# A fused attention and mixture-of-experts kernel: another written-out order, the last slot sums by halves, the first layer's banks opened earlier, the router's matrix stored in rows

## The chip, the cores and the metric

The kernel runs on one core of a Trainium2 chip. Its time is the device time of one execution in microseconds. The median of three runs of the kernel before is 344.75 us (343.94 to 345.07). One further execution was profiled; that one took 344.9 us, and the span of its trace is 343.1 us. All stretches below are counted from the start of that span.

## The reference

Two parts follow each other. The first is linear attention with a positive feature map for 8 batches, 8 heads, 576 tokens and a head dimension of 64:

```python
def phi(x):
    proj = np.einsum('bhsd,df->bhsf', x, w_phi)          # 64 -> 128 features
    proj = proj - np.max(np.abs(proj), axis=-1, keepdims=True)
    return np.concatenate([np.exp(proj), np.exp(-proj)], axis=-1)
q_p, k_p = (phi(q), phi(k))
kv = np.einsum('bhsf,bhsd->bhfd', k_p, v);  z = np.sum(k_p, axis=2)
num = np.einsum('bhsf,bhfd->bhsd', q_p, kv)
den = np.einsum('bhsf,bhf->bhs', q_p, z)[..., None] + 1e-06
x = num / den                                            # then reshaped to 4608 x 512
```

The second is a soft mixture of experts over the 4608 tokens with 32 slots, 8 experts of 4 slots each. The router's logits are normalised once over the tokens (to make the slots' inputs) and once over the slots (to mix the slots' outputs back):

```python
logits = x @ phi                                         # phi: 512 x 32
d = softmax(logits, over tokens);  slot_input = d.T @ x  # 32 x 512
h = np.maximum(slot_input[e] @ w1[e], 0.0);  slot_out[e] = h @ w2[e]   # 1024 hidden, per expert
c = softmax(logits, over slots);   out = c @ slot_out    # 4608 x 512
```

All inputs and outputs are float32.

## The kernel before, in words

**Attention, the main loop.** Two batches are taken together, so there are 32 units (4 batch pairs by 8 heads) of 1152 tokens, which are 9 tiles of 128 tokens. 72 blocks of four tiles pass through `proj` (line 264: one block of keys and one of queries, the queries two blocks behind), the exponentials on ScalarE (`kneg_exp`, `kpos_exp`, `qpos`, `qneg`, lines 295 to 334), the maxima on VectorE (`kmax` 269, `qabs` 326), the scaling of the values on GpSimd (`vals` 284), the sums of keys by values (`kvmm` 311) and the numerators (`num` 364, three to a unit), which VectorE (`scale` 375, `comb` 380) and GpSimd (`divide` 406) turn into rows of x.

**The slots, interleaved.** When enough of x stands, its tiles are turned by TensorE, multiplied by the router's matrix, and the exponentials' sums over tokens are added to a running accumulator `acc` (names `turn`, `logits`, `gmax`, `gexp`, `dturn`, `slotsum`, `update`). The last three groups have functions of their own, whose names begin with z. In `zsum` (559) group 0 and 1 are summed into one PSUM bank and group 2 into another, each as matmuls of 512 columns; `zup` (564) adds a bank to `acc` in two halves of 256 columns. `zone` makes the correction of the maxima, `zst` (602, 604) multiplies `acc` by it into one bank `st` of five times 32 columns, and `zsi` (607) copies that to `si`, the slots' inputs, in two halves. `si` lies in the place of the router's matrix `phs`. `layer1` (841) multiplies `si` by the first weights.

**The way back to the tokens.** For the first three groups of 512 tokens `tfour` (617, GpSimd) spreads the mixing weights, `tturn` (626) turns them on TensorE into a PSUM bank, `tcopy` (630, ScalarE) copies that bank and `trest` (636, VectorE) subtracts the copy from it in its upper half. The other six groups go through `repeated` and `combine` later.

**Experts and output.** After the planned part the rest is written out: `layer1` of experts 4 to 7, `lastw`, `hidden`, `picked`, `layer2` (935) for both halves of the output columns, `slots2`, and `output` (959, 960), which writes 18 tiles of 512 KB. There, TensorE's order is that of the text.

**Transfers.** All go through SyncE's queue, in the order in which they are issued: 512 KB for each two blocks of keys and queries (`load`), 325 KB for each unit of values (`vload`), the constants and the router's matrix (`consts`), and 64 weights of 512 KB. 26 of these weights (`weight`) have room from the start; others follow when pools of the main loop close (`close`).

**The order.** Everything from the first `proj` to the last `trest` is a list of tasks. A string `ORDER` holds one letter for each task, in the order in which the instructions are issued; every engine executes its own in that order. `Plan.run` takes the letters one by one. It also hands out numbered buffers, the tokens: a task that names one in `get` takes the first free number, and a `put` gives it back. `pr` is the token for the three PSUM banks z0, z1 and z2 of the pool `fin["pr"]`, `pl` that for two other banks, `nm` with `mo` or `psn` that for the three banks `nm0` to `nm2`. The figures for cost and latency in the task list were used by the program that searched the order; the kernel that runs takes nothing from them. A tile in a bank can be written anew when all readers of the tile before it in the same bank have ended.

At the end of the kernel before, the order of TensorE is: first of the three `tturn` between the first two `zdt`, second one after `zsum` 2, then `zst` 0 and 1, four `layer1` steps, the third `tturn`, and then the written-out part from `layer1(1, ...)` on.

Of the kernel before, what the change touches and what calls it, by code (L numbers as in the profile page):

```python
# [21 lines left out]
CH = 3  # L22
# [34 lines left out]
class Plan:  # L57
# [42 lines left out]
ORDER = (  # L100
    "abbccdaebfdebgehijeefechigcjdklfdmehinoelkgnfjgchiajmoljfcpnhldikqrdnlggjfsmoqahibtlukjcvmojwvcnfpdqrwlvkqnhislm"
    "oxbkwftcghyvjqwfzdiaAqhxnjbmolAvxgdikjcvpwrwlqdgmojsqfklAahinbtgcmojvvwcydkzlwgfnqrpjdqhismolAfnAtcvkAwmolynghij"
    "vfqawzbhlAvqkpjwmocdiAvgcjbnfxdlrnAqghidlkwsfyjmoqzhitalkjcvmowpvcgbnjxdlrqwAdfqnhilgvkjwksqfAaAmoljmotchiygvpzv"
    "cAwfnjhqwrnlqvAkdilfwgsymoAqhztkdicjmovwcdkAagbAnlgjfbvrqpjwflshimoAqvdtlkwvgnhijqywajmolvqwzcvAwApcyAbdkxzlnfxA"
    "xgnfqAjmoBhiBhACcCkdiBmodrBCcgsfjqhinatCblkjvnmoDvrwlEqwFBpvgBfwslCqhtkdicjmoCcbdkgnfBjvBhiCyljGnwqrqmovClvgwkzH"
    "dDmosfchiItEpwjcFbnagHJIdJnAgKAlAqfyjrqvwlkzvahidmoqsjflgLkAhicpjmowvcwbntxqdAyAGlnkfdqhivlgvfwjwkjqmohilvcmoLwp"
    "yzMcbnfAagdlxrjdqgksqAmoAnlhitkjvfcwamojzvhilAngqfMjNdpcrwvlghidqjkslkAaAwfbnyqthimoljvmozKcgpjwvcbnfAhwlqrAdiAq"
    "vgsklmodtkcwgjnfvqmojbdxlwganhiyqzvrAwcpAkjsfldhiAmoqvnNtflwgvkyjwhiqjmolvqzwAcvAAwpcybfznaAlxOkxxBdfxBmonCqCkBd"
    "hiBgCrjcgsCqmobfltkPvhiAnDjhajdicxAEgwjFlvnqfwpBvmodBrwlCgqCjshiqktcmoyvjvcGbfwanBwkBnldCrCqdmolzkhiHgDImojfcEhi"
    "spcFbvnHwJIydtJnAAKrlAqdfqvklwgLhijGsmoqggMvfLljzwkvhicApmowjcbdantqfdAlAkOhiyqvggwjmolznAfavNkqwjmolvhicjpOcbnf"  # L110
    "AwlrdqksglfjnhiAamoqKyhtlzkdijcmoMvvpAwcgNnAAdqrjwlfvqdkwglmosjkhiyqajznftxlbhivcgvmowjpcbnfxAwlrdqAAdgqkPshilmo"
    "vtnfcjwhivkqwybfnqgvhjzmoldikAcmopAvgrwjcdsqfbAgahilwtnyqvfjwlahvnkdiqmokwlcmopjvzOcAkwAdgymlAzdfAqgnofjBgnhiBrj"
    "cCCajsBxxBntxlxCCAPhidArqvjDvkwfwlgEmoqFBvkBhimocCpwCsctBBCldqjnqyvkajnlbCxwrvxqxfblgvkwzHhidDIfwJmoEsFcApGyhitH"
    "ljIqfnmoJGKgAhzckAdijvqdlwakvbgnmoqfjLKglhiAwmocArpjvcsbfAqwnytldkvqgdhijlwfajnxgmozvqAhiwkMlcApmoAvjcnfwlkdrqnN"
    "qsmohildgtfjcvkywaLhizblvAgnmoqApwjfcvArdjlwksqhiqmodytzcnfgvhijlwknAmovqArwjlvkwcpsymoAlgqzntcAkvdAQjRwQnSqSqvk"
    "wrQOQSgfljshiSAvTmomoUlVQpwQRUSyqtSPQvqSwTzvAyQVAzMwqSyQRvzQwSWyASAzTAAXRXXYYYZVZ0Z0W10W2W2P341567483N489642+8-3"
    "4*796-49//5R//=+=<<>O!*P1!!!5+*")
# [8 lines left out]
def tile_kernel(ctx: ExitStack, tc, xT, vv, w, phi, w1, w2, cst, out):  # L126
# [471 lines left out]
    def zst(i):  # L598
        sf = fin["sf"]
        if i == 0:  # L600
            fin["st"] = bank3("zst", [128, KC + 1, NS], "pst")
            nc.tensor.matmul(fin["st"][:, KC, 0:1], sf.rearrange("p a s -> p (a s)"), ssum, start=True, stop=True)
        for kc in (2 * i, 2 * i + 1):
            nc.tensor.matmul(fin["st"][:, kc], acc[:, kc * 128:(kc + 1) * 128], sf[:, 0], start=True, stop=True)
# [50 lines left out]
    for b in range(NB + 2):  # L655
        def task(kind, engine, cost, fn, key, bank, **k):
            add(kind, key, engine, cost, lambda: fn(key), at=4 / 3 * bank, **k)
        task("proj", PE, 0.99 if 1 < b < NB else 0.77, proj, b, b, after=[("load", b // 2)], lat=0.27, mode="r", get=["psk"] * (b < NB) + ["psq"] * (b > 1), put=["xs"] * (b % 2))
        bank = [f"kb{b % 2}"]
        if b < NB:  # L660
            task("kmax", DVE, 0.6, kmax, b, b, after=[("proj", b)], get=["mk"] + bank, put=bank, lat=0.13)
            task("kfac", ACT, 0.19, kfac, b, b, after=[("kmax", b)])
# [3 lines left out]
        for p, (b_, u, t0, t1) in enumerate(pieces):  # L666
            if b_ == b:
# [7 lines left out]
                     get=["pkv"] * (t0 == 0), put=["kf", "vs"] * end, mode="c", lat=0.22)  # L675
        q, bank = b - 2, [f"qb{b % 2}"]
        if q >= 0:
            task("qabs", DVE, 0.63, qabs, q, q, after=[("proj", b)], get=bank, put=bank, lat=0.13)
# [4 lines left out]
    for s in range(NK):  # L683
# [9 lines left out]
        if end:  # L693
# [6 lines left out]
        task("num", PE, 0.71, num, after=[("qneg", (CH * s + CH - 1) // 4), ("kvcopy", u)], get=["psn", ("nm", ("num", s))],  # L700
             put=["qf"] * any(t % 4 == 3 for t in range(CH * s, CH * s + CH)) + ["kvs"] * end, mode="c", lat=0.22)
        task("scale", DVE, 0.272, scale, after=[("num", s), ("qsquare", u)], get=[] if c else ["un"])
        task("comb", DVE, 0.272, comb, after=[("scale", s)], put=["psn", ("nm", ("num", s))])
# [64 lines left out]
        task("dturn", PE, 0.32, dturn, n, after=[("gexp", n)], get=hold("dturn", n), put=["lT"], mode="f")  # L768
# [23 lines left out]
    def close(k):  # L792
# [5 lines left out]
            ("u", [("divide", (NU - 1, 2))]), ("c", [("zsum", 2), ("zlog", 2)])]  # L798
# [7 lines left out]
    for c in range(NCH):  # L806
        bk = "pr" if c == 2 else "pl"
        last("zturn", c, PE, mode="f", cost=(0.466, 0.14, 0.466)[c], fn=lambda c=c: zturn(c), after=opens + [("divide", (NU - 1, c))] + [("flogits", (i, 0, 1, 2)) for i in last_of], get=[("pr", ("x", c))])
        d = pick("zcopy") == "d"
        last("zcopy", c, DVE if d else ACT, (0.07 + 0.1335 * len(zj(c))) if d else 0.05 + 0.107 * len(zj(c)), lambda c=c, d=d: zcopy(c, d), after=[("zturn", c)], get=[("xT", ("z", c))], put=[("pr", ("x", c))])  # L810
        last("zlog", c, PE, 0.45, lambda c=c: zlog(c), mode="s", after=[("zcopy", c), ("part", (last_of[c], 0, 1, 2))], get=[(bk, ("l", c))], put=[("xT", ("z", c))])
        last("zmax", c, DVE, 0.46, lambda c=c: zmax(c), after=[("zlog", c)])
# [15 lines left out]
    for i in range(2):  # L828
        last("zst", i, PE, 0.59, lambda i=i: zst(i), after=[("zup", 2 + i), ("zone", 5), ("zss", 1)], get=[] if i else ["mo", ("nm", "zst")])
# [22 lines left out]
    last("hopen", 0, None, 0.0, hopen, after=[("zsi", 1)] + [("zspin", i) for i in range(NFIN)] + [("zlt", c) for c in range(NCH)], lat=0.0)  # L852
# [184 lines left out]
```

## Time and profile before

| what | value |
|---|---|
| median of three runs | 344.75 us |
| profiled execution, its own time | 344.9 us |
| its span | 343.1 us |
| TensorE busy, share of the span | 327.2 us, 95% |
| VectorE, ScalarE, GpSimd | 243.6, 233.2, 168.0 us |
| data moved | 74.09 MB, mean 216 GB/s |
| main loop, last `flogits` begins at | 272.75 us |
| `layer1` begins at | 284.17 us |
| last matmul ends at | 332.83 us |

The table's last three rows are from the timeline of TensorE. In a row of the timeline stand the start and the duration in us, the engine, the line, the operation with its tiles, the number of instructions, and in brackets how long the engine was idle before and what released it. "issue" there means that no wait in the profile explains the idle time. In a row of the table by windows stand, for each engine, its busy time and its instructions, then the granted clock of TensorE (PEclk), the share of the DMA engines' time and the rate in GB/s. PEld is TensorE's weight load, which runs beside the matmuls.

### The profile page before, as it was taken

To read this page: it belongs to the slowest core of one execution; us is meant where nothing else is said; L and a number is where in the kernel's file an instruction comes from. 1 tells how busy PE (TensorE), PEld (TensorE's weight loads), DVE (VectorE), ACT (ScalarE), POOL (GpSimd) and SP (SyncE) were. 2 spreads that over 40 slices of the span, in tenths; PEclk is the share of its full clock that TensorE was granted. 3 is DMA by queue.
4 is the path that set the end of the run, shared out by engine and by line. 5 is a ranking of instruction groups with operands and counts; after the bars stand their busy time and mean duration, and the time that the engine had idled before them with its cause. 6 is when DMAs were issued, how large, how long until landed. Compare 5 with 4: busy or idle time off the path is not lost.

```text
span 343.1 us, 16153 instructions
## 1 busy us (share of the span) xinstructions
PE 327.2 (95%) x6825; PEld 271.1 (79%) x6825; DVE 243.6 (71%) x683; ACT 233.2 (68%) x677; POOL 168.0 (49%) x353
## 2 busy tenths in 40 slices
PE   8997999999999999999999999999999999999970
PEld 4896899998979999998899998979998753355430
DVE  1576487987787888887888888688886562615780
ACT  3897489968867888777789978677886250204470
POOL 1546466872356867561758758256664511130000
PEclk9999899999999999999999999999999999999995
DMA  6377256267234654674262844495426979998698
GB/s 223 117 238 257 83 196 226 67 208 285 66 111 155 204 166 165 210 302 118 58 195 61 320 154 149 162 319 176 128 76 233 352 297 406 408 406 333 282 400 324
DMA packets 22649, 74.09 MB, mean 216 GB/s; under 512 B 2992, under 2 KB 3248, under 8 KB 22576
## 3 DMA queue, kind: packets, MB, share of 16 engines
q1 hardware_dynamic: 22576, 73.05, 60.1%
q8 instruction: 54, 0.88, 1.0%
q14 instruction: 19, 0.16, 0.1%
HBM read 63.60 MB, written 9.44 MB: 213 GB/s over the span
## 4 chain that ended last, share of the span: by engine, by line
PE 92%; DVE 2%; ACT 2%; issue 1%; POOL 1%; ACTq 0%; POOLq 0%
PE kvp L311 23%; PE psn L364 20%; PE psq L264 12%; PE psk L264 10%; PE psx L734 5%; PE yp L935 4%; PE hp L841 4%; PE pso L959 3%; PE psl L417 2%; PE pss L456 2%; PE psw L183 1%; PE psc L921 1%; PE psd L449 1%; PE pss L559 1%; PE psh L903 1%
## 5 line engine op out<-in xcount | busy, mean ns | idle before, releaser
L284 POOL TENSOR_TENSOR vs<-vt,mk 128x520 f32<-128x520 f32 (+3 forms) x128 | 91.6, 730 | 63.3 <-ACT mk L273 42.6
L311 PE MATMUL kvp<-vs,kf 128*64 128x65 f32 (+1 forms) x2304 | 93.3, 230 | 1.9 <-issue 1.9
L311 PEld LDWEIGHTS kvp<-vs,kf 128*64 128x64 f32 x2304 | 81.8, 138 | 9.3 <-issue 5.4
L364 PE MATMUL psn<-kvs,qf 128*64 128x65 f32 x2304 | 82.1, 222 | 0.8 <-issue 0.8
L264 PE MATMUL psq<-xs,wd 64*128 64x128 f32 x576 | 78.7, 284 | 0.0
L264 PE MATMUL psk<-wd,xs 64*128 64x128 f32 x576 | 77.4, 283 | 0.6 <-ACT kf L298 0.4
L364 PEld LDWEIGHTS psn<-kvs,qf 128*64 128x64 f32 x2304 | 74.5, 138 | 3.4 <-issue 1.4
L264 PEld LDWEIGHTS psq<-xs,wd 64*128 64x128 f32 x576 | 69.2, 190 | 3.7 <-issue 1.1
L264 PEld LDWEIGHTS psk<-wd,xs 64*128 64x128 f32 x576 | 68.4, 190 | 4.1 <-ACT kf L298 1.3
L269 DVE TENSOR_REDUCE mk<-psk 128x4 f32<-128x512 f32 x72 | 48.4, 678 | 17.2 <-PE psk L264 8.0
L331 ACT ACTIVATE qf<-psq 128x512 f32<-128x512 f32 x72 | 42.7, 595 | 20.0 <-DVE mts L326 5.9
L326 DVE TRANSPOSE_TENSOR_REDUCE mts<-psq 128x16 f32<-128x512 f32 x72 | 50.7, 706 | 7.6 <-PE psk L264 3.6
L295 ACT ACTIVATE kf<-psk 128x512 f32<-128x512 f32 x72 | 42.6, 592 | 18.7 <-DVE mk L269 7.6
L406 POOL TENSOR_TENSOR xc<-un,dn 128x256 f32<-128x256 f32 x64 | 39.2, 614 | 12.6 <-PE pss L456 6.6
L375 DVE TENSOR_TENSOR un<-psn,eq 128x195 f32<-128x195 f32 x96 | 33.1, 348 | 16.3 <-PE psn L364 12.6
L334 ACT ACTIVATE qf<-psq 128x512 f32<-128x512 f32 x72 | 42.9, 601 | 0.4 <-DVE mts L326 0.2
L298 ACT ACTIVATE kf<-psk 128x512 f32<-128x512 f32 x72 | 42.6, 596 | 0.0
L342 ACT ACTIVATE mh<-mts 32x36 f32<-32x36 f32 x128 | 29.4, 230 | 7.5 <-DVE mts L326 5.9
L380 DVE TENSOR_TENSOR un<-psn,un 128x195 f32<-128x195 f32 x96 | 33.2, 349 | 1.1
L348 DVE TENSOR_REDUCE eq<-mh 32x9 f32<-32x36 f32 x128 | 26.4, 206 | 2.6 <-ACT mh L342 1.1
L272 ACT ACTIVATE mk<-mk 128x4 f32<-128x4 f32 x72 | 15.1, 210 | 4.0 <-DVE mk L269 3.4
L351 POOL TENSOR_TENSOR eq<-eq 128x9 f32<-128x9 f32 x32 | 6.5, 203 | 22.0 <-DVE eq L348 22.0
(130 smaller groups left out, 342.4 us busy)
## 6 DMA issues: line engine op xcount, KB each, us to landing
wt<-w SPq DMA_DIRECT2D x64, 512.0 KB, 7.0
xs<-xT SPq DMA_DIRECT2D x36, 512.0 KB, 4.2
vt<-vv SPq DMA_DIRECT2D x32, 325.0 KB, 3.3
out<-o SPq DMA_DIRECT2D x18, 512.0 KB, 3.7
xs<-xT SPq DMA_DIRECT2D x2, 128.0 KB, 2.5
cs<-cst SPq DMA_DIRECT2D x1, 128.5 KB, 4.0
wd<-w SPq DMA_DIRECT2D x1, 64.0 KB, 2.1
phs<-phi SPq DMA_DIRECT2D x1, 64.0 KB, 3.8
```

What stands on the lines that cost most here:

```text
L264: nc.tensor.matmul(ps, l, r, start=True, stop=True)
L269: nc.vector.tensor_reduce(km[b][:, 2], kx[b], axis=AX, op=ALU.max, apply_absolute_value=True)
L284: nc.gpsimd.tensor_tensor(vs[b][:, :, place(b, u, t, o):place(b, u, t, o) + n], v[:, t + o:t + o + n].unsqueeze(1).broadcast_to([128, 2, n ...
L295: nc.scalar.activation(kf[b][:, 1], kx[b], AF.Exp, scale=-1.0)
L298: nc.scalar.activation(kf[b][:, 0], kx[b], AF.Exp)
L311: nc.tensor.matmul(ps[f:f + FE // 2, pn, o:o + m], kf[b][:, pn, NT * u + t - 4 * b, f:f + FE // 2], v2[:, pn, at:at + m], start=(t == 0 an ...
L326: nc.vector.tensor_reduce(mts.rearrange("p r j -> p j r")[:, o:o + 4], qx[b].rearrange("p j (r t) -> p (j r) t", t=32), axis=AX, op=ALU.ma ...
L331: nc.scalar.activation(qf[b][:, 0], qx[b], AF.Exp)
L334: nc.scalar.activation(qf[b][:, 1], qx[b], AF.Exp, scale=-1.0)
L364: nc.tensor.matmul(ps[64 * f:64 * f + 64, j, pn], q2[:, pn, 64 * f:64 * f + 64], kv[:, pn, b2], start=True, stop=True)
L380: nc.vector.tensor_tensor(x, nx.pop(s)[:, :, 1], x, op=ALU.add)
L406: nc.gpsimd.tensor_tensor(x[:, :, h * D:(h + 1) * D], un[u][:, a:b, 0:64], dn[u][:, a:b].unsqueeze(2).broadcast_to([128, b - a, 64]), op=A ...
```

## The change

Four things change.

1. `ORDER` and the table of its letters are new throughout: 1824 letters in place of 1823. The work of the main loop is the same.
2. `zsum` of group 2 is two tasks, each with all four row groups but only half of the 512 columns, in the same bank. `zup` 2 waits, in the list, for the first half alone; in the new order the second half is issued ahead of it.
3. `st` lies in a bank of `pr` in place of one of `nm`; it isn't given back. `hopen`, which opens the pools of the first layer's accumulators, waits for `zup` 1 and `zone` 3 in place of `zsi` 1, and stands ahead of `zsum` 3. The first `layer1` step stands between `zsi` 0 and `zsi` 1.
4. The host stores the router's matrix as 128 rows of 512 bytes; it was 512 pieces of 128 bytes for the same transfer of 64 KB.

The order of SyncE's queue differs too. The old one has `load` 4, `consts`, `weight` 0, `load` 5, `vload` 4, `weight` 1, `load` 6, `weight` 2, `vload` 5; the new one has `load` 4, `vload` 2, `load` 5, `consts`, `vload` 3, `weight` 0, `vload` 4, `load` 6, `vload` 5, and `weight` 1 only behind `load` 9. At the end the new order has `zspin` 1 ahead of `zlog` 2, no `tturn` ahead of `layer1`, and after the four `layer1` steps three times `tturn`, `tcopy`, `trest`. Following the tokens through both orders, `tturn` 0, 1 and 2 take z2, z2 and z1 in the old one, and z1, z1 and z1 in the new one, where `st` keeps z0 and `zsum` 2 keeps z2.

The diff, without the table of letters and most of the two strings; the last line of each string is there. In the old one `/` is zup, `=` zst, `<` zsi, `>` hopen, `!` l1, `5` tturn, `+` tcopy, `*` trest; in the new one `+` is zup, `-` hopen, `*` zst, `/` zsi, `=` l1, `<` tturn, `>` tcopy, `!` trest, `7` zsum, `O` wsum and `P` wdiv.

```diff
 ORDER = (
...
-    "4*796-49//5R//=+=<<>O!*P1!!!5+*")
+    "585957++-7+Q+**/=/OP===<>!<>!<>!")
...
     def constants():
         nc.sync.dma_start(cs, cst)
-        nc.sync.dma_start(phs, phi.rearrange("(c p) s -> p c s", p=128))
+        nc.sync.dma_start(phs, phi.rearrange("p (c s) -> p c s", c=KC))
...
     def zsum(c):
-        if c != 1:
+
+        h, c = max(c - 2, 0), min(c, 2)
+        if c != 1 and not h:
             fin["sum", c // 2] = zbank("lr"[c == 2], ("s", c), [128, DM], "pss")
         ps = fin["sum", c // 2]
+        d = slice(h * DH, (h + 1) * DH) if c == 2 else slice(0, DM)
         for j in range(G):
-            nc.tensor.matmul(ps[32 * j:32 * j + 32], fin["d", c][:, j], tile4(last_of[c], j), start=c != 1, stop=c > 0,
+            nc.tensor.matmul(ps[32 * j:32 * j + 32, d], fin["d", c][:, j], tile4(last_of[c], j)[:, d], start=c != 1, stop=c > 0,
                              skip_group_check=True)
...
         if i == 0:
-            fin["st"] = bank3("zst", [128, KC + 1, NS], "pst")
+            fin["st"] = zbank("r", ("st", 0), [128, KC + 1, NS], "pst")
...
-        last("zsum", c, PE, 0.87, mode="s", fn=lambda c=c: zsum(c), after=[("zde", c)] + [("zsum", 0)] * (c == 1), get=[] if c == 1 else [(bk, ("s", c))], put=["de"])
+        for i in (2, 3) if c == 2 else (c,):
+            last("zsum", i, PE, 0.45 if c == 2 else 0.87, mode="s", fn=lambda i=i: zsum(i), after=[("zde", c)] + [("zsum", i - 1)] * (i % 2),
+                 get=[] if i % 2 else [(bk, ("s", c))], put=["de"] if i != 2 else [])
...
-            last("zup", 2 * i + h, DVE, 0.396, lambda i=i, h=h: zup(i, h), after=[("zsum", 1 + i), ("zco", i)], put=[("pl", ("s", 0))] if h and not i else [])
+            last("zup", 2 * i + h, DVE, 0.396, lambda i=i, h=h: zup(i, h), after=[("zsum", 1 + i + h * i), ("zco", i)], put=[("pl", ("s", 0))] if h and not i else [])
...
-        last("zst", i, PE, 0.59, lambda i=i: zst(i), after=[("zup", 2 + i), ("zone", 5), ("zss", 1)], get=[] if i else ["mo", ("nm", "zst")])
+        last("zst", i, PE, 0.59, lambda i=i: zst(i), after=[("zup", 2 + i), ("zone", 5), ("zss", 1)], get=[] if i else [("pr", ("st", 0))])
...
-    last("hopen", 0, None, 0.0, hopen, after=[("zsi", 1)] + [("zspin", i) for i in range(NFIN)] + [("zlt", c) for c in range(NCH)], lat=0.0)
+    last("hopen", 0, None, 0.0, hopen, after=[("zup", 1), ("zone", 3)] + [("zspin", i) for i in range(NFIN)] + [("zlt", c) for c in range(NCH)], lat=0.0)
...
-    arrays = dict(xT=xT, vv=vv, w=np.concatenate([w_phi, w_phi]), phi=c(moe_phi), w1=c(moe_w1),
+    arrays = dict(xT=xT, vv=vv, w=np.concatenate([w_phi, w_phi]), phi=c(moe_phi.reshape(KC, 128, NS).transpose(1, 0, 2)).reshape(128, KC * NS), w1=c(moe_w1),
```

The other changed lines give the search other figures for costs and latencies.

More of the change, by code (lines that the diff above doesn't have):

```diff
@@ L102 @@
[L102 to L106, printed above, removed]
@@ L657, in task @@
             add(kind, key, engine, cost, lambda: fn(key), at=4 / 3 * bank, **k)
-        task("proj", PE, 0.99 if 1 < b < NB else 0.77, proj, b, b, after=[("load", b // 2)], lat=0.27, mode="r", get=["psk"] * (b < NB) + ["psq"] * (b > 1), put=["xs"] * (b % 2))
+        task("proj", PE, 0.896 if 1 < b < NB else 0.77, proj, b, b, after=[("load", b // 2)], lat=0.34, mode="r", get=["psk"] * (b < NB) + ["psq"] * (b > 1), put=["xs"] * (b % 2))
         bank = [f"kb{b % 2}"]
         if b < NB:
-            task("kmax", DVE, 0.6, kmax, b, b, after=[("proj", b)], get=["mk"] + bank, put=bank, lat=0.13)
-            task("kfac", ACT, 0.19, kfac, b, b, after=[("kmax", b)])
+            task("kmax", DVE, 0.6, kmax, b, b, after=[("proj", b)], get=["mk"] + bank, put=bank, lat=0.16)
+            task("kfac", ACT, 0.19, kfac, b, b, after=[("kmax", b)], lat=0.21)
             task("kneg_exp", ACT, 0.478, kneg_exp, b, b, after=[("proj", b)], get=["kf"] + bank, put=bank, lat=0.13)
@@ L699, in tile_kernel @@
             task("qsquare", POOL, 0.61, qsquare, u, after=[("qmin", u)])
-        task("num", PE, 0.71, num, after=[("qneg", (CH * s + CH - 1) // 4), ("kvcopy", u)], get=["psn", ("nm", ("num", s))],
-             put=["qf"] * any(t % 4 == 3 for t in range(CH * s, CH * s + CH)) + ["kvs"] * end, mode="c", lat=0.22)
+        task("num", PE, 0.70, num, after=[("qneg", (CH * s + CH - 1) // 4), ("kvcopy", u)], get=["psn", ("nm", ("num", s))],
+             put=["qf"] * any(t % 4 == 3 for t in range(CH * s, CH * s + CH)) + ["kvs"] * end, mode="n", lat=0.22)
         task("scale", DVE, 0.272, scale, after=[("num", s), ("qsquare", u)], get=[] if c else ["un"])
-        task("comb", DVE, 0.272, comb, after=[("scale", s)], put=["psn", ("nm", ("num", s))])
+        task("comb", DVE, 0.272, comb, after=[("scale", s)], lat=0.22, put=["psn", ("nm", ("num", s))])
         for t in ((CH * c, CH * c + CH),) if u == NU - 1 else ((0, NT),) if end else ():
@@ L767, in dturn @@
             turned(lTs.pop(n), ps[:, 1])
-        task("dturn", PE, 0.32, dturn, n, after=[("gexp", n)], get=hold("dturn", n), put=["lT"], mode="f")
+        task("dturn", PE, 0.28, dturn, n, after=[("gexp", n)], get=hold("dturn", n), put=["lT"], mode="f")
         def dcopy(n, got=got):
```

39 lines of the change are left out of this document (22 added, 17 removed), and 10 rows, old and new, of the table LETTERS.

## The prediction, made before the changed kernel was run

> **What bounds the kernel now.** I read the page first, then tables by windows, then the timelines of TensorE, SyncE, ScalarE and VectorE at the places that the change touches.
>
> ```profile
> PE 327.2 (95%) x6825; PEld 271.1 (79%) x6825; DVE 243.6 (71%) x683; ACT 233.2 (68%) x677; POOL 168.0 (49%) x353
> ...
> PEclk9999899999999999999999999999999999999995
> ...
> q8 instruction: 54, 0.88, 1.0%
> ```
>
> TensorE is busy for 95% of the span and no other engine comes near. So an order can gain only where TensorE idles, runs at a lower clock, or does less. Where is that?
>
> ```profile
> 20.00:40.00 20.00, 17.28 (x378) 0.91 0.73 244
> 40.00:60.00 20.00, 20.00 (x540) 1.00 0.55 182
> 60.00:80.00 20.00, 20.00 (x482) 1.00 0.52 174
> 80.00:100.00 20.00, 20.00 (x438) 1.00 0.40 135
> ...
> 40.00:180.00 140.00, 140.00 (x3416) 129.42 (x3413) 115.14 (x325) 113.73 (x343) 86.40 (x179) 1.00 0.51 168
> 180.00:260.00 80.00, 79.44 (x1882) 72.74 (x1878) 66.47 (x186) 64.04 (x191) 51.08 (x110) 1.00 0.50 166
> 284.17:324.00 39.83, 39.83 (x439) 18.13 (x439) 18.18 (x62) 9.59 (x19) 6.18 (x10) 1.00 0.92 369
> ```
>
> The first four rows are of TensorE alone: busy time, matmuls, granted clock, DMA share, GB/s. From 40 to 260 us it loses 0.56 us (79.44 of 80.00), and from the first layer to 324 nothing. What is lost lies at 20 to 40 us: 378 matmuls, where the next three windows have 487 in the mean. The 109 that are missing are worth 109 / 24.3 per us = 4.5 us.
>
> **The early loss.** In the timeline of TensorE, then by windows with all engines (two matmuls are counted per product of two float32 tiles):
>
> ```profile
> 26.04 1.38 PE L364 MATMUL psn<-kvs,qf 128*64 128x65 f32 x38
> 28.23 0.51 PE L364 MATMUL psn<-kvs,qf 128*64 128x65 f32 x10 [0.81 <-issue]
> ...
> 32.14 0.86 PE L311 MATMUL kvp<-vs,kf 128*64 128x65 f32 x22
> 34.92 1.25 PE L311 MATMUL kvp<-vs,kf 128*64 128x65 f32 x10 [1.92 <-issue]
> ```
> ```profile
> 19.50:25.60 6.10, 6.10 (x152) 5.84 (x148) 4.76 (x15) 5.50 (x17) 2.43 (x7) 1.00 1.00 321
> ...
> 28.25:32.50 4.25, 4.25 (x120) 4.06 (x121) 2.33 (x8) 3.17 (x12) 2.55 (x4) 1.00 1.00 342
> ...
> 28.20:34.90 6.70, 4.78 (x128) 4.44 (x127) 3.83 (x12) 4.48 (x15) 3.29 (x6) 1.00 0.94 315
> ...
> 35.07:38.48 3.41, 3.41 (x32) 3.07 (x32) 0.28 (x1) 0.17 (x1) 1.22 (x2) 0.50 0.44 151
> ```
>
> Both pauses lie inside a task (38 is 24 + 14 matmuls, 22 isn't a multiple of 8), so no operand is waited for. Between them stand 128 matmuls and 127 loads, 255 instructions; and 2 x 6825 instructions over the 54 packets of the instruction queue are 253 to a packet. I take it that TensorE ran out of instructions twice, at neighbouring blocks. Both come when the DMA engines had been full for some time (share 1.00). SyncE's queue shows why they were full:
>
> ```profile
> 19.09 0.38 SPq L171 DMA_DIRECT2D xs<-xT  x1
> ...
> 20.46 0.51 SPq L235 DMA_DIRECT2D wt<-w  x1
> 21.07 0.38 SPq L171 DMA_DIRECT2D xs<-xT  x1
> 26.45 0.33 SPq L175 DMA_DIRECT2D vt<-vv  x1
> ...
> 27.88 0.42 SPq L235 DMA_DIRECT2D wt<-w  x1
> ```
>
> Two bursts: `load`, `consts`, `weight`, `load` (1.7 MB) and `vload`, `weight`, `load`, `weight` (1.9 MB), each about 5 us of transfer at 321 to 342 GB/s. The pauses cost, from the last start to the next (a matmul lasts 0.22): 28.23 - 27.20 - 0.05 = 0.98 and 34.92 - 32.78 - 0.05 = 2.09. Behind the second the clock is granted at 0.50 for 3.41 us, worth 1.71. Sum 4.8 us, near the 4.5 of the counts.
>
> **Part 1, the new order.** It has one `weight` in place of three in this stage, and at most 0.84 MB (`vload` and one transfer of 512 KB) or `load` and `consts` (0.7 MB) together, some 2.5 us. So both pauses and the slow clock go: -4.8, between 0 (the pauses have another cause) and -4.8. The weights that leave must come later. The new order's fullest run there is `vload` 26, `weight` 19, `load` 30 and 31, `weight` 20 (2.4 MB); the old one has `vload` 28, `load` 32, three weights and `load` 33 (2.9 MB) without a loss above the 0.56 us. A late block costs between 0 and 3.8 (the second pause with its clock); I take one small pause, +0.8, by the 0.81 that stands in the row. What data the new order makes TensorE wait for can't be seen in the old trace: between -0.56 (all that is lost from 40 to 260) and +1.9 (the longest idle time of TensorE in the trace); I take +0.2, since DVE and ACT have about 30% to spare. And the changes between kinds of matmul:
>
> ```profile
> 60.79 0.27 PE L264 MATMUL psq<-xs,wd 64*128 64x128 f32 x1
> ...
> 60.90 0.27 PE L264 MATMUL psq<-xs,wd 64*128 64x128 f32 x1
> 61.10 0.28 PE L364 MATMUL psn<-kvs,qf 128*64 128x65 f32 x2
> ```
>
> 0.11 within `proj`, 0.20 at its end: 0.09 more. The orders have 74 such ends and beginnings against 60, but 26 against 33 neighbouring `proj`, which change row groups, and more single spins: 0 to -0.6, taken as -0.1. The main loop: -4.8 + 0.8 + 0.2 - 0.1 = **-3.9**.
>
> **Part 2, up to the first layer.** TensorE, then VectorE:
>
> ```profile
> 276.67 0.82 PE L641 MATMUL psw<-cs 128*128 128x512 bf16 x3
> ...
> 278.13 0.66 PE L626 MATMUL psc<-cs,xT 128*128 128x128 f32 x4
> 278.62 0.27 PE L449 MATMUL psd<-cs,eT 128*128 128x128 f32 x1
> ...
> 282.10 0.65 PE L626 MATMUL psc<-cs,xT 128*128 128x128 f32 x4
> 282.59 0.28 PE L602 MATMUL pst<-ssum,sf 128*128 128x1 f32 x2
> 282.77 1.08 PE L604 MATMUL pst<-sf,acc 128*128 128x32 f32 x8
> 284.17 7.07 PE L841 MATMUL hp<-wt,phs 128*32 128x512 f32 x64 [0.32 <-DVE phs L607]
> ```
> ```profile
> 281.41 1.70 DVE L564 SCALAR_TENSOR_TENSOR acc<-acc,co,pss 128x256 f32<-128x256 f32 x4
> ...
> 283.89 0.36 DVE L607 COPY phs<-pst 128x64 f32<-128x64 f32 x2 [0.78 <-PE pst L604]
> ```
>
> Two `tturn` leave this chain, 0.49 each (278.13 to 278.62, 282.10 to 282.59). The second leaves a hole, since `zst` then waits for the four `zup`, which begin at most 0.49 earlier plus what the shorter queues of ScalarE and VectorE give. Between -0.49 and -0.98, taken as **-0.6**. The halves of `zsum` give 0: both lie in one bank, and the second is issued ahead of `zup` 2. That a bank is waited for as a whole is seen in the row at 283.89: the first copy needs `zst` 0 alone, yet starts at the end of the eighth matmul (282.77 + 1.08 = 283.85). If the half counted, `zup` 2 could come 0.4 (1.70 / 4) earlier, but VectorE is then still in `zup` 1. `hopen` gives 0: `layer1` starts 0.1 us behind the first copy (0.36 / 2) as it is. A `zspin` ahead of `zlog` 2 is covered by the maxima on VectorE; uncovered it is 0.27 (0.82 / 3). The router's matrix in rows: 0, as it is read long after its load; the whole load's 64 KB are 0.2 us at 321 GB/s.
>
> [...]
>
> **Part 3, behind the first layer's steps.** `zsum` 2 keeps z2 and `st` keeps z0, so the three `tturn` share z1: each waits for the `trest` before it. Behind a waiting `tturn` stands all of TensorE's queue, `layer1(1, ...)` first. The old third `tturn`, with ScalarE and VectorE, shows one round:
>
> ```profile
> 291.18 0.66 PE L626 MATMUL psc<-cs,xT 128*128 128x128 f32 x4
> 291.76 1.06 PE L841 MATMUL hp<-wt,phs 128*32 128x512 f32 x8
> ```
> ```profile
> 291.39 0.69 ACT L894 ACTIVATE hs<-hp,rs 128x512 f32<-128x512 f32 x1 [8.01 <-PE hp L841]
> 291.98 0.58 ACT L630 CAST xT<-psc 128x512 fp32r<-128x512 f32 x1
> ...
> 292.89 0.69 DVE L636 TENSOR_TENSOR xT<-psc,xT 64x512 fp32r<-64x512 f32 x1
> ```
>
> From 291.18 to 292.89 + 0.69 = 293.58 are 2.40 us, in which `hidden` gets ahead on ScalarE and VectorE. A round without it is 0.66 + 0.58 + 0.69 and three hand-overs of 0.04 (283.89 - 283.85) = 2.05. Two rounds, 4.45 us (4.1 to 4.8), come ahead of the third `tturn`. Its 0.58 was there before, and the two moved turns are inside the rounds. In these rounds TensorE idles 1.74 + 1.39 us. The 2.09 us of the early pause were followed by 3.41 us at clock 0.50, the 0.98 us by none. So the clock costs between 0 and 1.71 more; I take 0.7, as it may not come and would partly lie over the second wait. Nothing behind absorbs this, since TensorE has no idle time to 324 and the last nine output tiles wait for it. Together **+4.45 + 0.7**.
>
> **The sum**, from the profiled execution's 344.9: -3.9 - 0.6 + 4.45 + 0.7 = +0.65, 345.55. The median of the runs shown is 0.15 lower: **345.4**.
>
> **The rivals.** *The pauses stay or come back* at other full runs: slower. For it: the cause is inferred, and no view dates a packet of instructions. Against: 255 instructions apart, both behind a burst. Then 344.75 - 0.6 + 4.45 + 0.7 = 349.3; the point is whether TensorE shows two waits for "issue" over 0.8. [...]
>
> *The turns don't wait*, because banks come free otherwise than I read: 344.75 - 3.9 - 0.6 = 340.3. Against it are the tokens, z1 three times.
>
> *The order's own waits* reach the bound of 1.9: 345.4 + 1.7 = 347.1. For it: the order is new throughout. Against: VectorE and ScalarE idle for 29% and 32% of the span, so a small delay there is made up.
>
> *Full gain, cheap turns*: no new pause, clock stays, rounds of 2.05: 345.4 - 0.8 - 0.7 - 0.35 - 0.2 = 343.3.
>
> **Chances.** Forecast 0.46, alone 344.2 to 346.6; pauses stay 0.11; no wait at the turns 0.12; order's waits 0.17; cheap turns 0.14. A measurement can tell some 0.3%, 1.03 us. Faster than 343.7: 0.12 + 0.14 + 0.02 of the forecast's = 0.28. Slower than 345.8: 0.11 + 0.17 + 0.10 of the forecast's = 0.38. Within: 0.34. The range leaves out most of the two outer rivals: 342.4 to 348.2.
>
> **What will show it.** Right: in 20 to 40 us about 480 matmuls at clock 1.00 and no "issue" of 0.8 us; behind the 64 `layer1` matmuls three rows of L626, the second and third with 1.4 to 1.8 us idle, released by VectorE's L636; perhaps clock 0.50 behind; `layer1` beginning 4.5 us earlier than 284.17. Wrong: turns in one row without idle time, or "issue" waits at the DMA-full stretches.

## The result, and the profile after

The changed kernel takes 347.47 us (median of 20 runs, 344.54 to 349.89); the kernel before, timed beside it, 344.43 us (20 runs, 340.96 to 347.12). The ratio is 1.0098, with a 95% interval of 1.0075 to 1.0122: slower by 3.0 us. The ratios, here and below, leave out single executions that took over 1.5% more than the fastest of their kernel; the medians include them. The forecast was 345.4, with 344.2 to 346.6 for itself alone and 342.4 to 348.2 in all. The profiled execution took 347.5 us with a span of 345.7, which is 2.6 more than before.

The page of the changed kernel, busy times and granted clock:

```profile
PE 326.8 (95%) x6833; PEld 270.1 (78%) x6833; DVE 244.7 (71%) x683; ACT 235.1 (68%) x677; POOL 168.2 (49%) x353
...
PEclk9999999999999999999999999999999999999995
```

TensorE is busy for 0.4 us less in a span that is 2.6 us longer, and no slice up to the last matmul has a lower clock. So the changed kernel waits more. Its table by windows, TensorE alone (busy time, matmuls, granted clock, DMA share, GB/s):

```profile
20.00:40.00 20.00, 20.00 (x519) 1.00 0.53 166
40.00:180.00 140.00, 138.87 (x3377) 1.00 0.55 178
180.00:260.00 80.00, 79.76 (x1920) 1.00 0.53 176
```

The 378 matmuls of the first row have become 519, without a pause. The two others have lost 1.37 us (before: 0.56). The timeline of TensorE from the last `flogits` on shows where the gain goes:

```profile
268.21 0.92 PE L417 MATMUL psl<-xT,phs 128*32 128x128 f32 x24
...
273.20 0.30 PE L423 MATMUL psl<-part,cs 128*32 128x128 f32 x2 [0.87 <-issue]
...
279.02 1.08 PE L607 MATMUL pst<-sf,acc 128*128 128x32 f32 x8 [0.29 <-DVE acc L567]
280.42 7.07 PE L846 MATMUL hp<-wt,phs 128*32 128x512 f32 x64 [0.32 <-DVE phs L610]
287.42 0.66 PE L629 MATMUL psc<-cs,xT 128*128 128x128 f32 x4
288.01 1.90 PE L846 MATMUL hp<-wt,phs 128*32 128x512 f32 x10
289.98 0.63 PE L629 MATMUL psc<-cs,xT 128*128 128x128 f32 x4
290.54 1.06 PE L846 MATMUL hp<-wt,phs 128*32 128x512 f32 x6
291.53 0.33 PE L449 MATMUL psL<-cs,part 128*128 128x128 f32 x1
293.38 0.63 PE L629 MATMUL psc<-cs,xT 128*128 128x128 f32 x4 [1.52 <-DVE xT L639]
295.74 0.44 PE L449 MATMUL psL<-cs,part 128*128 128x128 f32 x2 [1.73 <-DVE xT L639]
296.11 1.92 PE L846 MATMUL hp<-wt,phs 128*32 128x512 f32 x16
```

Line 629 is `tturn`, 639 `trest`, 846 `layer1`, 449 the turning of the last logits (`lastw`). The turns do wait for `trest`, but not as the forecast had it: only the third one idles. Between the first and the second turn TensorE has work: the matmuls of the next section, `layer1(1, (0,))`, stand in its queue five ahead of the second turn and three behind it (10 and 6 rows, two per matmul). So TensorE's order there isn't that of the text, contrary to what the description of the kernel ahead of the prediction says. The second wait for `trest` falls on the second `psL`, which takes bank z1 too.

With the stretches of both kernels side by side, from the rows of the two timelines, and with a second profile of the changed kernel that was taken later ("again", below):

| stretch | before | changed | changed, again |
|---|---|---|---|
| start to last `flogits` | 272.75 | 268.21 | 267.85 |
| to the first `layer1` | 11.42 | 12.21 | 11.15 |
| to `layer1(1, (1,))` | 9.93 | 15.69 | 15.94 |
| to the end of the last matmul | 38.73 | 38.75 | 40.97 |
| to the end of the span | 10.27 | 10.84 | 10.89 |

So the main loop gives 4.5 to 4.9 us and the turns take 5.8 to 6.0; the rest differs between two executions of the same kernel.

### The profile page after: what moved, and what is told of

Same layout as the page of the kernel before. It is cut to its first block, busy times and chain, and to the rows that moved or that the text cites. A ratio compares the mean times of both kernels' runs of the same rounds, so it can differ in the third digit from the quotient of the medians.

```text
span 345.7 us, 16179 instructions
## 1 busy us (share of the span) xinstructions
PE 326.8 (95%) x6833; PEld 270.1 (78%) x6833; DVE 244.7 (71%) x683; ACT 235.1 (68%) x677; POOL 168.2 (49%) x353
## 4 chain that ended last, share of the span: by engine, by line
PE 88%; ACT 3%; DVE 3%; DMA 2%; issue 1%; POOL 1%; ACTq 0%; POOLq 0%
PE kvp L311 22%; PE psn L364 19%; PE psq L264 11%; PE psk L264 9%; PE psx L737 4%; PE hp L846 4%; PE yp L940 4%; PE pso L964 3%; PE psl L417 2%; DMA xs<-xT 2%; PE pss L456 2%; PE psw L183 1%; PE psc L926 1%; PE psd L449 1%; PE psh L908 1%
## 5 line engine op out<-in xcount | busy, mean ns | idle before, releaser
L364 PE MATMUL psn<-kvs,qf 128*64 128x65 f32 x2304 | 80.0, 222 | 0.6 <-issue 0.6
L364 PEld LDWEIGHTS psn<-kvs,qf 128*64 128x64 f32 x2304 | 73.5, 138 | 3.3 <-issue 2.1
L264 PE MATMUL psq<-xs,wd 64*128 64x128 f32 x576 | 75.6, 280 | 0.1
L264 PE MATMUL psk<-wd,xs 64*128 64x128 f32 x576 | 75.3, 281 | 0.3 <-DMA xs<-xT 0.2
L264 PEld LDWEIGHTS psq<-xs,wd 64*128 64x128 f32 x576 | 67.5, 187 | 3.4 <-ACT kf L298 0.8
L264 PEld LDWEIGHTS psk<-wd,xs 64*128 64x128 f32 x576 | 67.4, 188 | 3.3 <-issue 2.1
L406 POOL TENSOR_TENSOR xc<-un,dn 128x256 f32<-128x256 f32 x64 | 39.2, 616 | 10.8 <-DVE dn L391 8.1
L387 POOL TENSOR_TENSOR dn<-eq,un 128x9 f32<-128x9 f32 (+1 forms) x34 | 7.1, 208 | 27.7 <-DVE un L380 26.2
```

The source lines that it names most:

```text
L264: nc.tensor.matmul(ps, l, r, start=True, stop=True)
L364: nc.tensor.matmul(ps[64 * f:64 * f + 64, j, pn], q2[:, pn, 64 * f:64 * f + 64], kv[:, pn, b2], start=True, stop=True)
L406: nc.gpsimd.tensor_tensor(x[:, :, h * D:(h + 1) * D], un[u][:, a:b, 0:64], dn[u][:, a:b].unsqueeze(2).broadcast_to([128, b - a, 64]), op=A ...
```

## The experiments

Each kernel was timed beside the kernel before; the ratios are to that one.

| run | median, us | ratio, 95% interval |
|---|---|---|
| new main loop, old end | 340.43 | 0.9891 (0.9852 to 0.9929) |
| old main loop, new end | 350.77 | 1.0173 (1.0136 to 1.0211) |
| turns spread | 340.77 | 0.9894 (0.9857 to 0.9931) |
| before, weights late | 341.50 | 0.9914 (0.9884 to 0.9944) |
| changed, again | 348.41 | 1.0133 (1.0098 to 1.0168) |
| turns spread, weights early | 342.50 | 0.9960 (0.9930 to 0.9989) |
| turns spread, parts undone | 340.97 | 0.9928 (0.9907 to 0.9950) |
| turns spread, fewer warming matmuls | 341.77 | 0.9935 (0.9905 to 0.9966) |
| changed, a bank of its own for one turn | 343.60 | 1.0002 (0.9974 to 1.0030) |
| changed, useless matmuls in the waits | 349.85 | 1.0176 (1.0129 to 1.0223) |
| turns spread, one ahead of `zst` | 340.45 | 0.9912 (0.9880 to 0.9945) |

### The order cut in two

The two orders were cut at the first `zturn` and their halves exchanged. The first kernel is the one before with the new main loop, in the old letters (the first line of many):

```diff
 ORDER = (
-    "abbccdaebfdebgehijeefechigcjdklfdmehinoelkgnfjgchiajmoljfcpnhldikqrdnlggjfsmoqahibtlukjcvmojwvcnfpdqrwlvkqnhislm"
+    "abbbccdeafdebgehiejefechigcjdknglbkdfenljfhiajmoelmocphigcjdknlfbnguqrjlfajshihqtmodilkvcvmowpxgcnfjdlrqwnqkvgwl"
...
```

> The kernel before, with the changed kernel's order up to the first zturn and its own order and code behind it. If the gain of the new order lies in the main loop (the two early pauses and the half clock gone, 4.5 to 5.7 us) and its loss behind the last zturn: 339.5 to 341, ratio 0.986 to 0.990, with some 480 matmuls or more at clock 1.00 from 20 to 40 us. If the early pauses come back elsewhere, or the new main loop has waits of its own that eat the gain: 343.5 to 345, ratio 0.997 to 1.002.

340.43 us, ratio 0.9891. Its windows and its timeline of TensorE:

```profile
20.00:40.00 20.00, 20.00 (x518) 1.00 0.54 166
```
```profile
267.00 0.92 PE L417 MATMUL psl<-xT,phs 128*32 128x128 f32 x24
...
278.41 7.91 PE L841 MATMUL hp<-wt,phs 128*32 128x512 f32 x66 [0.32 <-DVE phs L607]
```

The new main loop alone is worth 4.0 us, in spite of 0.84 us that its end loses by accident: here one matmul of `layer1(1, (0,))` has got ahead of the first layer's 32 (66 rows, 7.91 us, where 64 take 7.07).

The second kernel is the changed one with the old main loop, in the new letters:

```diff
 ORDER = (
-    "abbbccdeafdebgehiejefechigcjdklgmbkdfelmjfhiajnoemnocphigcjdklmfblgqrsjmfajthihrunodimkvcvnowpxgclfjdmsrwlrkvgwm"
+    "abbccdaebfdebgehijeefechigcjdkmfdnehiloemkglfjgchiajnomjfcplhmdikrsdlmggjftnorahibumqkjcvnojwvclfpdrswmvkrlhitmn"
...
```

> The changed kernel, with the order of before up to the first zturn and its own order and code behind it. If the end costs what the two traces show (0.8 up to the first layer, 5.8 at the turns, 0.6 behind): 351 to 352, ratio 1.019 to 1.022, with both early pauses. By the prediction's terms for these parts (-0.6 and +4.45): 348.3, ratio 1.011. If the wait for an instruction in zlog is an accident of this one order: 350.5.

350.77 us, ratio 1.0173, which is 6.0 us slower than before. That is less than the traces of the two kernels give (0.8 + 5.8 + 0.6 = 7.2) and far above the 3.9 of the prediction's terms. It is near the 350.5 expected for the case that the wait of 0.87 us in `zlog` (the logits of the last groups) is an accident of one order, and here that wait is missing. Its timeline of TensorE:

```profile
28.74 0.51 PE L364 MATMUL psn<-kvs,qf 128*64 128x65 f32 x10 [1.11 <-issue]
35.43 0.78 PE L311 MATMUL kvp<-vs,kf 128*64 128x65 f32 x10 [1.92 <-issue]
...
298.36 0.69 PE L449 MATMUL psL<-cs,part 128*128 128x128 f32 x2 [1.74 <-DVE xT L639]
298.98 3.27 PE L846 MATMUL hp<-wt,phs 128*32 128x512 f32 x16
```

Both early pauses stand where they did. Two things are new. Behind the pause of 1.92 us the ten matmuls take 0.78 us, where the same ten, behind the same 1.92 us, took 1.25 in the profile of before: this time the clock didn't fall (granted 1.00 from 28 to 36 us). And behind the waits at the end it did: 16 rows of `layer1` take 3.27 us for 1.92 (granted 0.54 from 298.3 to 302 us).

### The early pauses: bursts of transfers

In the kernel before the first three weights were moved out of the two bursts, and nothing else (x is `weight`, c is `proj`; each line is a piece of the string):

```diff
-    "oxbkwftcghyvjqwfzdiaAqhxnjbmolAvxgdikjcvpw
+    "obkwftcghyvjqwfzdiaAqhnjbmolAvgdikjcvpw
...
-    htkdicjmoCcbdkgnf
+    htkdixcjmoCcbdkgnf
...
-    mosfchiItEpwj
+    mosfxchiItEpwj
...
-    spcFbvnHwJIydtJ
+    spxcFbvnHwJIydtJ
```

> The kernel before, its first three weights taken out of the stretch from 20 to 30 us and issued ahead of proj 25, 27 and 46; nothing else. If TensorE runs out of instructions behind the two bursts of transfers: no pause of 0.8 us or more from 20 to 40 us, clock 1.00 there, 340 to 341, ratio 0.986 to 0.990. If the pauses have another cause: both stay, 344 to 345, ratio 0.998 to 1.002.

341.50 us, ratio 0.9914, 0.5 us above the range expected if bursts are the cause. The window, and then SyncE's queue and TensorE further on:

```profile
20.00:40.00 20.00, 20.00 (x508) 1.00 0.52 169
```
```profile
183.06 1.45 SPq L235 DMA_DIRECT2D wt<-w  x1
184.60 1.09 SPq L171 DMA_DIRECT2D xs<-xT  x2
185.74 0.42 SPq L235 DMA_DIRECT2D wt<-w  x1
```
```profile
194.72 0.37 PE L264 MATMUL psk<-wd,xs 64*128 64x128 f32 x1 [1.39 <-issue]
```

The early pauses are gone, with 2.9 us of the 4.0 that the new main loop is worth (the intervals of the two ratios overlap). A part of the rest may be the pause of 1.39 us at 194.72: a new one, inside a `proj`, behind two weights and two loads that now come together. The reverse was done to the changed kernel with its turns spread (next part): two weights back around the load at 25 us (b), and two of the three behind `vload` 7 taken out.

```diff
-    "ftjkhidyruanobjmgvnow
+    "ftjkhidyruanoxbxjmgvnow
...
-    ghiruanoxjmvkxywxcjnoz
+    ghiruanojmvkywxcjnoz
```

> The changed kernel with its turns spread (340.8), two of its weights issued around the load at 25 us, as before had them, and no longer in the run of transfers at 46 to 51 us; nothing else. If bursts of transfers starve TensorE of instructions: a wait for issue of 0.8 to 2.1 us between 27 and 36 us, with or without the half clock, 342 to 345. If it doesn't hang on the bursts: 340.3 to 341.3 and no such wait.

342.50 us against 340.97 and 341.77 for two others of the family on the same chip at the same time. The intervals of the ratios overlap, so the times alone don't decide; the timeline does. SyncE's queue, then TensorE's timeline:

```profile
25.16 0.44 SPq L235 DMA_DIRECT2D wt<-w  x1
25.64 0.43 SPq L171 DMA_DIRECT2D xs<-xT  x1
26.12 0.43 SPq L235 DMA_DIRECT2D wt<-w  x1
```
```profile
33.38 0.37 PE L264 MATMUL psq<-xs,wd 64*128 64x128 f32 x1 [1.24 <-issue]
```

A pause of 1.24 us for "issue", some 6 us behind the burst. None of the nine profiles with the new main loop and without this burst has a pause from 20 to 40 us. Bursts taken away take the pauses away (one profile), and one put in brings one (one profile): that bursts bring on the early pauses is shown. That it is the fetching of instructions that they delay is still inferred, as no view dates those packets.

A burst isn't enough for a pause, though. The new order has one of 1.9 MB as well, at 47 us: a `vload` and three weights, followed at 52 us by a `vload` and two loads. Behind it the first profile of the changed kernel shows a pause of 0.59 us, at 58.18. The second shows none, at the same DMA share from 40 to 180 us, 0.55. What else is needed stays open. The profile with early weights has a second pause for "issue" too, 0.8 us in `num`, that no run ties to a burst.

### The turns

Each turn was put behind a step of the first layer, in the changed kernel:

```diff
-    "585957++-7+Q+**/=/OP===<>!<>!<>!")
+    "585957++-7+Q+**/=/OP=<>!=<>!=<>!")
```

> The changed kernel, each tturn with its tcopy and trest behind a step of the first layer (steps 1, 2 and 3 of 0 to 3) in place of all three behind the last. If the loss of the end is the wait for bank z1 (1.52 + 1.73 us) and the four column groups that are broken up as five and three matmuls of layer1(1, 0) (2.96 us for what takes 1.92): both go, 347.5 - 4.3 = 343.2, ratio 0.996, and layer1(1, (1,)) begins some 11.2 us behind the first layer, not 15.7. If the turns only move the wait into the first layer (each step of 1.7 us shorter than a round of 2.05): up to 1 us comes back, 344.2. If the loss has another cause: 346.5 to 347.5, ratio 1.006 to 1.009.

340.77 us: 6.7 us faster than the changed kernel, where 4.3 were expected. Its timeline of TensorE:

```profile
266.45 0.92 PE L417 MATMUL psl<-xT,phs 128*32 128x128 f32 x24
...
277.60 3.64 PE L846 MATMUL hp<-wt,phs 128*32 128x512 f32 x32 [0.32 <-DVE phs L610]
281.17 0.65 PE L629 MATMUL psc<-cs,xT 128*128 128x128 f32 x4
281.76 1.92 PE L846 MATMUL hp<-wt,phs 128*32 128x512 f32 x16
...
288.97 1.92 PE L846 MATMUL hp<-wt,phs 128*32 128x512 f32 x16
```

No turn waits, and each group of 16 rows takes 1.92 us. From 277.60 to 288.97 are 11.37 us, 4.32 less than the 15.69 of the changed kernel: the term itself was right. To see where the other 2.4 us come from, the changed kernel was run once more.

> The changed kernel once more, unaltered, for a second profile beside the runs that follow. Its time: 347 to 348. If the wait of 0.87 us in zlog and the first matmuls of full speed at 6.9 us are of the order, both come again; if they are accidents of one execution, one or both are missing, and the profile is up to 2 us shorter. If the two waits at the turns can take the clock with them, as in the run with the old main loop (16 matmuls of layer1 in 3.27 us at clock 0.54 where 1.92 is usual), this profile may show it: about 1.7 us more.

348.41 us, ratio 1.0133. Its timeline of TensorE and its windows (all engines; the clock is the third number from the end):

```profile
267.85 0.92 PE L417 MATMUL psl<-xT,phs 128*32 128x128 f32 x24
...
279.00 7.08 PE L846 MATMUL hp<-wt,phs 128*32 128x512 f32 x64 [0.32 <-DVE phs L610]
...
294.94 3.64 PE L846 MATMUL hp<-wt,phs 128*32 128x512 f32 x16
298.52 1.59 PE L908 MATMUL psh<-cs,hs 128*128 128x128 f32 x8
```
```profile
294.40:297.80 3.40, 3.40 (x18) 0.81 (x18) 2.76 (x14) 0.51 (x2) 0.00 (x0) 0.50 1.03 411
```

Here the pause of 0.87 us in `zlog` is missing, and the first layer begins 11.15 us behind the last `flogits`, as with the turns spread. In its place the clock falls to 0.50 behind the waits at the turns: 1.72 us in `layer1` and 0.50 in `psh` (the turning in `picked`), and the second `psL` takes 0.69 for 0.44. Against this execution (span 346.8) the one with the turns spread (338.6) is 8.2 us shorter: 4.57 at the turns, 2.2 of half clock, 1.4 ahead of the last `flogits`.

Next, one of the three turns got a bank of its own, with the list of tasks unaltered:

```diff
     def tturn(g):
-        ps = fin["c", g] = zbank("r", ("c", g), [128, 4, 128], "psc")
+        ps = zbank("r", ("c", g), [128, 4, 128], "psc") if g != 1 else pmo.tile([128, 4, 128], F32, tag="nm0", name="psc")
+        fin["c", g] = ps
```

> The changed kernel, its second tturn given another bank (the one that zone used) in place of z1; the order is unaltered. If the turns wait for each other because they share z1: the 1.52 us ahead of the third turn go, and of the 1.73 us ahead of the second psL a part stays, since the third turn's trest still holds z1; with the shorter waits the clock stays at 1.00: 344 to 346 against 347.5 to 348.4. If something else than the bank holds the turns (tcopy, the queue of VectorE): 347 to 348.5.

343.60 us, ratio 1.0002. Its timeline of TensorE (630 is `tturn` here, 640 `trest`, 847 `layer1`):

```profile
288.28 0.66 PE L630 MATMUL psc<-cs,xT 128*128 128x128 f32 x4
...
291.61 0.44 PE L449 MATMUL psL<-cs,part 128*128 128x128 f32 x2 [1.43 <-DVE xT L640]
291.98 1.92 PE L847 MATMUL hp<-wt,phs 128*32 128x512 f32 x16
```

The wait of 1.52 us is gone, and of the 1.73 ahead of `psL` 1.43 stay, since the third turn still holds z1. It is the bank that the turns wait for. The row of 1.92 us shows a full clock (granted 1.00 from 280 to 300 us). The time is below the 344 to 346 expected. From the first layer (278.42) to `layer1(1, (1,))` are 13.56 us, 2.1 less than the 15.69 of the changed kernel; what else made this run faster lies in parts that differ between executions, the start (299 matmuls in the first 20 us in place of 265), the pause in `zlog` and the half clock, and wasn't separated.

To see whether the idle time is what lowers the clock, useless matmuls were put into the waits:

```diff
     def tturn(g):
+        for _ in range(7 if g else 0):
+            s = pmo.tile([128, 512], F32, tag="nm0", name="psw")
+            x = cs[:, 0:256].bitcast(mybir.dt.bfloat16)
+            nc.tensor.matmul(s, x[:, 0:128], x, start=True, stop=True)
```

> The changed kernel with seven matmuls of no use (bf16, 0.22 us each) ahead of the second and of the third tturn, in the time that TensorE would wait for bank z1. If the half clock behind the waits comes from the idle time: no stretch under 1.00 behind 280 us, layer1(1, (1,)) in 1.92 us where it took 3.64 in the second profile of the changed kernel, 346 to 347.5 in all since the waits stay. If the clock falls for another reason: half clock again, 348 or more.

349.85 us, which by the expectation would speak for another reason than the idle time. But the run doesn't answer the question. The useless matmuls took 0.42 us each (2.98 us for the seven ahead of the third turn), not 0.22, and so lengthened the chain; of the first seven, three fell between the matmuls of `layer1`; and the wait ahead of `psL` stayed outside them:

```profile
298.01 0.44 PE L449 MATMUL psL<-cs,part 128*128 128x128 f32 x2 [1.46 <-DVE xT L643]
298.38 3.54 PE L850 MATMUL hp<-wt,phs 128*32 128x512 f32 x16
```

The half clock (granted 0.52 from 298.4 to 301.9 us) came behind a single wait of 1.46 us, where it hadn't come behind the 1.43 us of the run before. That idle time is what lowers the clock is therefore not shown by an experiment, only by where it happens. In all, five profiles have waits of 1.4 us or more at this place, and three of them a half clock behind; of the eight without such a wait (the kernel before among them) none has one there.

Last, the first turn was put ahead of `zst`, where TensorE waits 0.29 us for `zup`:

```diff
-    "585957++-7+Q+**/=/OP=<>!=<>!=<>!")
+    "585957++-7+Q+<**>/=/!OP==<>!=<>!")
```

> The changed kernel with its turns spread, and the first of them ahead of zst, where TensorE waits 0.29 us for the last zup. If the turn fills that wait: the first layer begins 0.2 to 0.3 later behind the last flogits and layer1(1, (1,)) 10.8 behind the first layer, in sum 0.3 faster than with the turns spread alone: 340.5. If the turn delays zst by its whole 0.49 and more: the same or up to 0.3 slower.

340.45 us. Its timeline of TensorE:

```profile
267.33 0.92 PE L417 MATMUL psl<-xT,phs 128*32 128x128 f32 x24
...
276.40 0.66 PE L629 MATMUL psc<-cs,xT 128*128 128x128 f32 x4
...
278.47 5.36 PE L846 MATMUL hp<-wt,phs 128*32 128x512 f32 x48 [0.32 <-DVE phs L610]
...
289.14 1.92 PE L846 MATMUL hp<-wt,phs 128*32 128x512 f32 x16
```

The first layer begins 11.14 us behind the last `flogits`, no later than without the turn, and `layer1(1, (1,))` 10.67 behind that: 0.7 us less than with the turns spread. By the intervals of the times the two can't be told apart. Both beat both kernels, by 0.9% to 1.1% the one before.

### The small parts

The halves of `zsum`, the early `hopen` with the first step between the two `zsi`, and the rows of the router's matrix were undone together, with the turns spread:

```diff
-    "585957++-7+Q+**/=/OP=<>!=<>!=<>!")
+    "5859577+++Q+**//-=OP=<>!=<>!=<>!")
...
     def zsum(c):
-        h, c = max(c - 2, 0), min(c, 2)
-        if c != 1 and not h:
+        if c == 3:
+            return
+        if c != 1:
...
-        nc.sync.dma_start(phs, phi.rearrange("p (c s) -> p c s", c=KC))
+        nc.sync.dma_start(phs, phi.rearrange("(c p) s -> p c s", p=128))
```

> The changed kernel with its turns spread (340.8), and zsum 2 whole again, the banks of the first layer opened behind the second zsi with its first step behind that, and the router's matrix loaded by columns. By the prediction all three are worth 0: 340.5 to 341.1, the first layer begins 11.1 to 11.2 us behind the last flogits. If the halves let zup begin earlier or the first step hides the second zsi: 0.3 to 0.7 slower, 341.1 to 341.5, with more idle time ahead of the first layer than the 0.32 us in its row.

340.97 us, in a comparison whose ratio, 0.9928, overlaps that of the turns spread. Its timeline of TensorE:

```profile
267.14 0.92 PE L417 MATMUL psl<-xT,phs 128*32 128x128 f32 x24
...
278.28 3.64 PE L846 MATMUL hp<-wt,phs 128*32 128x512 f32 x32 [0.32 <-DVE phs L610]
```

11.14 us, against 11.15 with the three parts in place. In this stretch they are worth nothing.

### The start

In the profile of the changed kernel the first `proj` begins 0.74 us later than before and runs longer; the third profile here is that of the turns spread, whose order is the same up to there. Before, changed, turns spread:

```profile
1.10 4.13 PE L183 MATMUL psw<-call 128*128 128x512 bf16 x11 [1.10 <-POOL call L179]
5.17 1.71 PE L264 MATMUL psk<-wd,xs 64*128 64x128 f32 x16
```
```profile
1.10 4.88 PE L183 MATMUL psw<-call 128*128 128x512 bf16 x11 [1.10 <-POOL call L179]
5.91 2.13 PE L264 MATMUL psk<-wd,xs 64*128 64x128 f32 x16
```
```profile
5.03 1.71 PE L264 MATMUL psk<-wd,xs 64*128 64x128 f32 x16
```

The same instructions take 4.13 or 4.88 us, and 1.71 or 2.13: it is the moment at which TensorE gets fast that differs, not the order. Only the times of the rows show that: the granted clock reads 1.00 from 1 to 9 us in the profiles of both kernels. Fewer warming matmuls might let `proj` begin at 5.0 in any case:

```diff
-NWARM = 11
+NWARM = 9
```

> The changed kernel with its turns spread (340.8) and 9 warming matmuls at the start in place of 11. The eleven end between 4.9 and 5.8 us, by when the clock rises, and the first proj could begin at 5.0. If the late rise only delays proj because the warming matmuls themselves last longer: proj always begins by 5.1 us, 0.3 to 0.8 faster in the mean, 340.0 to 340.5. If fewer matmuls let the clock rise later: 341 to 342.

341.77 us (340.05 to 344.08), no gain; the same family without it had 340.97 beside it. The row shows why:

```profile
5.05 2.18 PE L264 MATMUL psk<-wd,xs 64*128 64x128 f32 x16
```

`proj` does begin at 5.05, and then runs slowly for 2.18 us. What beginning earlier gives is lost again, as TensorE isn't yet fast.

## Why the prediction came out as it did

**The direction of each large part held.** The order removes the early pauses, and the bursts bring them on: the rival in which they stay (349.3) falls with the changed kernel's own row from 20 to 40 us and the two runs that moved the weights. The turns wait for z1: the rival in which they don't (340.3) falls with the bank of its own. The rival with the order's own waits (347.1) has nearly the measured time, but not for its reason: those waits came to 0.8 us (below). That with cheap turns (343.3) falls with the end, which alone costs 6.0 us. The forecast of 345.4 missed 347.47 by 2.1 us. That lies outside the forecast's own range (344.2 to 346.6) and inside the whole one, whose upper part was there for the rival with the order's own waits: that the range held is in part luck. The sum failed in these steps.

**"Two rounds, 4.45 us (4.1 to 4.8)".** The stretch grew by 5.76 and 6.01 us in the two profiles. The step took TensorE's order from the text: all turns first, each idle until the `trest` before it. The rows show one idle round, 1.52 us, since the five matmuls of the next section filled the other; but they fill it badly. `layer1` works in groups of four matmuls on four groups of 32 columns, and 5 + 3 take 1.90 + 1.06 us where 4 + 4 take 1.92, 1.04 more. And the step named who waits behind a turn, but not who takes the bank after the last one: the second `psL`, 1.73 us. With the two turns that moved here (1.2 us) these make up 5.5 of the 5.76.

**"So the clock costs between 0 and 1.71 more; I take 0.7".** The half clock does come behind these waits, but whether it comes is a matter of chance: 0 in one profile of the changed kernel, 2.2 us in the other. The bound was too low, since the half clock also reached `psh`. The same chance sits, unseen, in the first term: **"-4.8"** for the early pauses counted 1.71 us of half clock from one profiled execution, as if it came each time. In the run with the old main loop the same pause of 1.92 us was not followed by it. So the sum took off 1.71 where it may come and added 0.7 where it may come too. The new main loop with the old end is worth 4.0 us by the medians, which looks like the 3.9 of the sum. But that end loses 0.84 us by the stray matmul, so the main loop alone is worth about 4.8 (an estimate from these two): the agreement is in part luck.

**"Between -0.49 and -0.98, taken as -0.6".** The way to the first layer became 0.79 us longer in the first profile, by a pause of 0.87 us that is missing in the second, where it is 0.27 shorter. The first turn gave its 0.49. The second gave nothing, as the lower bound had it, since `zst` now waits 0.29 us for `zup`. And the `zspin` (a useless matmul) ahead of `zlog` 2 was taken as covered, but seems to be so only in part: the first `psd` behind it comes 4.97 us after the last `flogits` (272.82 in the second profile), where it came 4.81 after (277.56 before). "Layer1 beginning 4.5 us earlier" became 3.75, and 5.17 in the second profile.

**"One small pause, +0.8" and "+0.2".** From 40 to 260 us the changed kernel lost 1.37 us in place of 0.56, 0.8 more, against 1.0 predicted. In the second profile it lost 0.89, 0.3 more, and no single wait for "issue" there reached 0.2. So the size holds in one execution and was too high in the other.

**The parts taken as nothing** (halves, `hopen`, rows) are nothing in their stretch (11.14 against 11.15 us), and in the time within what the runs can tell.

**Not in the sum at all**: the start, up to 1.3 us between two executions (the first `proj` ends at 8.04 us in the first profile of the changed kernel, at 6.74 with the turns spread), and 0.6 us more between the last matmul and the end of the span. The latter is 10.3 to 10.5 in three profiles with the old end and 10.8 to 10.9 in those of the changed kernel and with the turns spread. But it is 10.5 with the old main loop and the new end, so it isn't the new end alone; the cause stays open.

## What to carry to other kernels

Where a bank is shared, follow it past its last user: the longer of the two waits (1.73 us) was that of the next section's first tile in the same bank. And read the order from a timeline or from the built program, not from the text: here matmuls of the next section had come ahead of a waiting turn. Here a turn whose bank passed through two other engines cost its own 0.6 us where some 1.8 us of other work stood ahead of the next user (turns spread), and 1.5 to 1.7 us more where that came at once (the changed kernel). And a loss that a single profile shows at half clock should be entered with the chance that it comes, on both sides of a sum.

## What the hardware did that was not expected

**The half clock comes or stays away behind the same wait.** 1.92 us: once followed by it (before, granted clock 0.50), once not (old main loop, 1.00). 1.43 and 1.46 us at the end: once not (own bank, 1.00), once yes (useless matmuls, 0.52). 1.52 and 1.73 (or 1.74) one after the other: once not (changed, 1.00), twice yes (changed again, 0.50; old main loop with the new end, 0.54). The start differs between executions too: the eleven warming matmuls take 3.99 us with the turns spread, 4.13 before, 4.88 and 4.87 in the two profiles of the changed kernel. What decides is not shown by any run.

**Pauses move.** The pauses for "issue" behind the new order's transfers lie at other places and have other lengths in each execution (0.59 us at 58.18 and 0.87 at 273.20 in one profile of the changed kernel, no such pause in the next). The two early ones of the old main loop came in both of its profiles (0.81 and 1.92 us; 1.11 and 1.92). The run with late weights is 2.9 us faster without the two pauses; that they are waits for instructions is inferred.

**Four column groups work at once.** 16 rows of `layer1`, which are eight matmuls, take 1.92 us in sets of four (turns spread); broken up as five and three matmuls they take 2.96 (changed). In the run with useless matmuls one such matmul alone (two rows, at 287.42) takes 1.04 us, and a set of four (eight rows, at 288.71) 1.06.
